# Batch 0 of a fused attention and MoE kernel: its second half in plain float32, and its weights converted over more steps

## The chip, the cores and the metric

The kernel is written for one core of a Trainium2 chip. The metric is the device time of one execution in microseconds (us). "TensorE" does the matrix products, "VectorE" and "ScalarE" the elementwise work, "GpSimd" a little of the rest; DMA transfers are started from the queue of SyncE (SP) and from GpSimd's.

## The reference

Three stages follow one another; B = 8 batches, 8 heads, 576 rows, 512 channels. Only the first two touch the change.

```python
proj = np.einsum('bhsd,df->bhsf', x, w_phi)           # x is q, then k
proj = proj - np.max(np.abs(proj), axis=-1, keepdims=True)
phi = np.concatenate([np.exp(proj), np.exp(-proj)], axis=-1)
...
kv = np.einsum('bhsf,bhsd->bhfd', k_p, v)
...
xk = mu_k * x + (1.0 - mu_k) * x_prev                 # x_prev: the row before
xr = mu_r * x + (1.0 - mu_r) * x_prev
k = np.maximum(xk @ w_k, 0.0)                         # 512 -> 1024
v = k * k @ w_v                                       # 1024 -> 512
r = 1.0 / (1.0 + np.exp(-(xr @ w_r)))                 # 512 -> 512
x = r * v
...
h = np.maximum(x @ w_in, 0.0)
...
return h * gate @ w_out
```

## The kernel before, in words

**Attention** runs in 32 blocks (`block(Pi)`), one for two heads of one batch; four blocks make a batch. In a block TensorE projects rows (`pk`, `pq`), turns tiles (`pt`, `px`, `pr`), sums keys with values (`pkv`) and makes the results (`pn`). VectorE takes the largest absolute value of each row (`mx`), subtracts it (`t`), and normalizes the results (`rd`, `xn`). ScalarE takes the exponentials (`kp`, `kr`, `qf`) and copies the turned results to `xT`.

**The MoE** (`moe(u)`) works on units: unit u is half of a batch, 288 rows, so batch 0 is units 0 and 1. A unit has 20 steps: eight of k (`psk`, four weight blocks of 128 by 128 each), and twice two of receptance (`psr`, four blocks each) and four of values (`psv`, two products of eight blocks each, and two steps in which VectorE multiplies). Its inputs are mixed from `xT` (`mix`: ScalarE scales, VectorE adds the scaled row before).

**Precision.** From unit 1 on, each weight block is multiplied three times in the reduced format fp32r (`mm3`): low weights by high inputs, high by low, high by high. Inputs, weights and squares of k must be split into high and low for that: a ScalarE copy rounds, a VectorE subtraction gives the rest (`ml`, `kl`, `split` for weights). Unit 0 takes one plain float32 matmul for each block, with the whole weight, which lies where the low half will be.

**The weights** arrive as float64 and are converted chunk by chunk, 20 chunks of 512 columns (`step`): SP loads `raw` (two buffers), ScalarE takes the high word (`h<-raw`), VectorE clamps, shifts and combines (four instructions, `h<-h`, `h<-h`, `h<-raw,h` twice), and SP moves the result to its place. `tick()` brings each chunk under way one stage further and starts the next. Ticks stand twice in each block from -1 to 6, at steps given by `WAT`, and in `want(n)`, which ticks until n + 2 chunks are ready.

**The order.** TensorE's instructions keep the order in which the code gives them; on the other engines a scheduler chooses the order. From block 4 on, `feed` hands MoE steps out between the blocks: 6, 6, 7 and 9 in blocks 4 to 7 (`SR`), then 10 in each. What is left of the MoE follows the last block, then the third stage.

Of the kernel before, what the change touches and what calls it, by code (L numbers as in the profile page):

```python
# [25 lines left out]

NS = 15

MS, SLOW, SR = 4, 8, {4: 6, 5: 6, 6: 7, 7: 9}

WAT = {4: (4, 10), 5: (3, 7, 11), 6: (3, 5, 7, 9)}
DS0 = 10
AHEAD = 2
HS = S // 2
V1 = D + 1

# [6 lines left out]
def fused_kernel(ctx: ExitStack, tc: tile.TileContext, qk, va, wphi, ones2, mu, wk, wv, wr, win, wout, cw, out):  # L43
# [33 lines left out]
    def f(x):  # L77
        return x.bitcast(F32)
# [78 lines left out]
    with ExitStack() as p1:  # L157
# [27 lines left out]
        def split(n=None):  # L185

            while n is None or cleft[0] < n:
                if half:
                    hs, ls = half.pop()
                    V.behind("tensor_tensor", ls, f(ls), f(hs), ALU.subtract)  # L190
                    cleft[0] += 1
                if whole and (n is None or cleft[0] < n):
# [5 lines left out]
        under, ready, whole, half, cleft = [], [0], [], [], [0]  # L198

        def tick():  # L200
            for at in (2, 1):
# [221 lines left out]
        def mix(u, j):  # L423

            b, hf = divmod(u, 2)
            o = hf * HS
            hi = main.tile([P, KC, HS], F32R if u else F32, tag="mh", bufs=2, name=f"mh{j}")
            if u == 0:
# [3 lines left out]
                return hi, hi  # L432
            lo = main.tile([P, KC, HS], F32R, tag="ml", bufs=2, name=f"ml{j}")
# [22 lines left out]

        def want(n):

            while ready[0] < min(n + AHEAD, 20):
                tick()  # L460

        def moe(u):
            b, hf = divmod(u, 2)

            def mm(ps, wh, wl, xh, xl, first, last):
                if u:
                    mm3(ps, wh, wl, xh, xl, first, last)
                else:
                    T.matmul(ps, f(wl), xh, start=first, stop=last)

            def need(n):
                want(n)
                if u:
                    split(n)
            o = hf * HS
            for j in range(2):
                while not mix_next(u, j):
                    yield
            xh, xl = mixed.pop((u, 0))
            k2 = []  # L480
            for fp in range(FC // 2):
                kf = tmps.tile([P, 2, HS], F32, tag="tmp", name="kf")
                for j in range(2):
                    ps = psm.tile([P, 512], F32, tag="mm", name="psk")[:, :HS]
                    fc = 2 * fp + j
                    need(fc + 1)
                    for c in range(KC):
                        w = slice(fc * DM + c * P, fc * DM + c * P + P)
                        mm(ps, wkh[:, w], wkl[:, w], xh[:, c], xl[:, c], c == 0, c == KC - 1)
                    A.activation(kf[:, j], ps, AF.Relu)  # L490
                    if u == 1:
                        split()
                    yield
                if u == 0:
                    kh = main.tile([P, 2, HS], F32, tag="kh", bufs=4, name="kh")
                    A.square(kh, kf)
                    k2.append((kh, kh))
                    continue
                if u == 1:
                    A.square(kf, kf)  # L500
                else:
                    V.tensor_tensor(kf, kf, kf, ALU.mult)
                kh = main.tile([P, 2, HS], F32R, tag="kh", bufs=4, name="kh")
                kl = main.tile([P, 2, HS], F32R, tag="kl", bufs=4, name="kl")
                A.copy(kh, kf)
                V.tensor_tensor(kl, kf, f(kh), ALU.subtract)
                k2.append((kh, kl))
            rh, rl = mixed.pop((u, 1))
            for mp in range(2):
                sg = main.tile([P, 2, HS], F32, tag="sg", bufs=1, name="sg")  # L510
                for j in range(2):
                    ps = psm.tile([P, 512], F32, tag="mm", name="psr")[:, :HS]
                    mc = 2 * mp + j
                    need(9 + 6 * mp + j)
                    for c in range(KC):
                        w = slice(mc * DM + c * P, mc * DM + c * P + P)
                        mm(ps, wrh[:, w], wrl[:, w], rh[:, c], rl[:, c], c == 0, c == KC - 1)
                    A.activation(sg[:, j], ps, AF.Tanh, scale=0.5)
                    if u == 1:
                        split()  # L520
                    yield
                mix_next(u + 1, mp)
                x2 = tmps.tile([P, 2, HS], F32, tag="tmp", name="x2")
                for j in range(2):
                    ps = psm.tile([P, 512], F32, tag="mm", name="psv")[:, :HS]
                    mc = 2 * mp + j
                    need(12 + 6 * mp + 2 * j)
                    for kc in range(FC):
                        w = slice(mc * DFF + kc * P, mc * DFF + kc * P + P)
                        kh, kl = k2[kc // 2]  # L530
                        mm(ps, wvh[:, w], wvl[:, w], kh[:, kc % 2], kl[:, kc % 2], kc == 0, kc == FC - 1)
                    if u < 2:
                        split()
                    yield
                    if u < 2:
                        split()
# [15 lines left out]
        load_v(1)  # L552

        def extras(Pi, n):
            if n in WAT.get(Pi, ()):
                tick()
            if Pi == 7 and n == 14:
                taps()
            if Pi >= DS0 and dsteps and n in (3, 11):
# [181 lines left out]
```

## Time and profile before

| | |
|---|---|
| median of 3 runs | 1233.19 us (1229.55 to 1234.22) |
| the profiled execution | 1230.63 us, of which the span of the trace is 1228.7 |
| mean granted clock of TensorE | 0.995 |
| busy in the span: TensorE, VectorE, ScalarE, GpSimd | 1207.6, 762.8, 697.2, 67.8 us |
| moved by DMA | 100.81 MB, 82 GB/s on the mean |

The time of the profiled execution is the span and what lies around it. An engine is busy while an instruction of it runs; the granted clock is 1.00 where TensorE runs at 2.4 GHz and 0.50 where it runs at 1.2 GHz.

### The profile page before, as it was taken

The numbers are of one execution on the slowest core, as the hardware profiler recorded it, in microseconds if no ns is written. First come the engines' busy times: TensorE is split into PE (matmuls) and PEld (weight loads), VectorE is DVE, ScalarE is ACT, GpSimd is POOL, SyncE is SP. The second block draws the span as 40 slices with busy tenths as digits, with TensorE's granted clock in tenths as the row PEclk, the third lists the DMA queues.
The fourth block names the chain that finished last, engine by engine and source line by source line (L and its number), as shares of the span: only waits on it lengthen the run. The fifth ranks groups of instructions, "written<-read, shape, count | busy, mean of one in ns | idle before, by whom it ended". The sixth has DMA issues, their size and how long they took to land.

```text
span 1228.7 us, 29049 instructions
## 1 busy us (share of the span) xinstructions
PE 1207.6 (98%) x11920; PEld 1139.4 (93%) x11920; DVE 762.8 (62%) x1584; ACT 697.2 (57%) x1644; POOL 67.8 (6%) x179
## 2 busy tenths in 40 slices
PE   7899999999999999999999999999999999999998
PEld 7778899999999999999999999998888888888887
DVE  7979776576765765767646534426555754475555
ACT  6766776565665664665645534426554655465554
POOL 0000000111110101111000000000000000000000
PEclk9989999999999999999999999999999999999999
DMA  6656213222322332333110004050122101210220
GB/s 205 220 188 205 94 42 89 86 92 77 120 78 84 105 111 85 93 86 104 50 52 22 12 21 157 20 188 8 55 63 62 32 32 63 62 44 20 63 62 31
DMA packets 58838, 100.81 MB, mean 82 GB/s; under 512 B 10321, under 2 KB 39121, under 8 KB 58705
## 3 DMA queue, kind: packets, MB, share of 16 engines
q1 hardware_dynamic: 45424, 73.41, 18.1%
q0 software_dynamic: 3920, 15.93, 4.4%
q10 hardware_dynamic: 9360, 9.61, 2.9%
q8 instruction: 94, 1.54, 0.5%
q14 instruction: 40, 0.32, 0.1%
HBM read 66.42 MB, written 27.26 MB: 76 GB/s over the span
## 4 chain that ended last, share of the span: by engine, by line
PE 90%; DVE 4%; DMA 3%; ACT 2%; issue 1%; SPq 0%; ACTq 0%
PE psh L150 5%; PE psh L152 5%; PE psh L151 5%; PE pkv L309 5%; PE psv L150 5%; PE psv L151 5%; PE psv L152 5%; PE psk L151 5%; PE psk L152 5%; PE psk L150 5%; PE pso L150 5%; PE pso L152 5%; PE pso L151 5%; PE pn L362 5%; PE psr L150 3%; PE psr L151 3%
## 5 line engine op out<-in xcount | busy, mean ns | idle before, releaser
L58 DVE SCALAR_TENSOR_TENSOR ct<-h,cw,ct 128x460 f32<-128x460 f32 (+2 forms) x160 | 111.4, 696 | 84.9 <-ACT ct L58 83.7
L150 PE MATMUL psv<-kh,wvl 128*128 128x288 f32 x480 | 141.9, 296 | 0.0
L151 PE MATMUL psk<-ml,wkh 128*128 128x288 f32 x480 | 141.6, 295 | 0.0
L151 PE MATMUL psv<-kl,wvh 128*128 128x288 f32 x480 | 141.5, 295 | 0.0
L152 PE MATMUL psk<-mh,wkh 128*128 128x288 f32 x480 | 141.5, 295 | 0.0
L152 PE MATMUL psv<-kh,wvh 128*128 128x288 f32 x480 | 141.5, 295 | 0.0
L150 PE MATMUL psk<-mh,wkl 128*128 128x288 f32 x480 | 140.9, 293 | 0.0
L152 PE MATMUL psh<-xh,wih 128*128 128x462 f32 (+1 forms) x320 | 118.9, 372 | 0.0
L151 PE MATMUL psh<-xl,wih 128*128 128x462 f32 (+1 forms) x320 | 118.8, 372 | 0.0
L151 PE MATMUL pso<-gl,woh 128*128 128x460 f32 (+1 forms) x320 | 118.0, 371 | 0.0
L152 PE MATMUL pso<-gh,woh 128*128 128x460 f32 (+1 forms) x320 | 118.0, 371 | 0.0
L58 ACT ACTIVATE kf<-psk 128x288 f32<-128x288 f32 x128 | 52.3, 408 | 108.1 <-PE psk L152 105.2
L150 PE MATMUL psh<-xh,wil 128*128 128x462 f32 (+1 forms) x320 | 107.4, 372 | 0.0
L150 PEld LDWEIGHTS psv<-kh,wvl 128*128 128x128 f32 x480 | 90.1, 188 | 0.8
L58 ACT ACTIVATE h<-psh 128x462 f32<-128x462 f32 (+3 forms) x128 | 47.9, 410 | 75.7 <-PE psh L152 74.5
L150 PEld LDWEIGHTS psk<-mh,wkl 128*128 128x128 f32 x480 | 90.2, 188 | 0.1
L151 PEld LDWEIGHTS psk<-ml,wkh 128*128 128x128 f32 x480 | 90.2, 188 | 0.0
L151 PEld LDWEIGHTS psv<-kl,wvh 128*128 128x128 f32 x480 | 90.2, 188 | 0.0
L152 PEld LDWEIGHTS psv<-kh,wvh 128*128 128x128 f32 x480 | 90.2, 188 | 0.0
L152 PEld LDWEIGHTS psk<-mh,wkh 128*128 128x128 f32 x480 | 90.2, 188 | 0.0
L58 DVE SCALAR_TENSOR_TENSOR x<-sg,psv 128x288 f32<-128x288 f32 x64 | 29.0, 453 | 95.9 <-PE psv L152 85.7
L58 DVE TENSOR_TENSOR kf<-kf 128x576 f32<-128x576 f32 x56 | 42.4, 758 | 74.1 <-ACT kf L58 74.1
(106 smaller groups left out, 2836.7 us busy)
## 6 DMA issues: line engine op xcount, KB each, us to landing
rqk<-qk POOLq DMA_DIRECT2D x27, 576.0 KB, 4.8
va<-va SPq DMA_DIRECT2D x32, 325.0 KB, 4.4
x2s<-x SPq DMA_DIRECT2D x32, 288.0 KB, 2.3
raw<-wk SPq DMA_DIRECT2D x8, 512.0 KB, 5.0
raw<-wv SPq DMA_DIRECT2D x8, 512.0 KB, 3.7
raw<-win SPq DMA_DIRECT2D x16, 256.0 KB, 2.9
raw<-wout SPq DMA_DIRECT2D x16, 256.0 KB, 3.0
x2r<-x2s ACTq DMA_DIRECT2D x16, 231.0 KB, 2.7
```

What stands on the lines that cost most here:

```text
L58: x = op(*a, **k)
L150: T.matmul(ps, wl, xh, start=first, stop=False)
L151: T.matmul(ps, wh, xl, start=False, stop=False)
L152: T.matmul(ps, wh, xh, start=False, stop=last)
L309: T.matmul(o[r:r + 64], k_[:, r:r + 64], v_, start=(i == 0), stop=(i == len(prods) - 1))
L362: T.matmul(pn[b_][64 * r:64 * r + 64, j], qf[h_][:, c, o:o + 64], kv[:, c, h_], start=(j == 0 and c == 0), stop=(j == 4 - b_ and c == 1))
```

## The change

Unit 1 takes plain float32 as unit 0 does, and the two units go together (`moe_first`): k of unit 0, k of unit 1, then for each pair of output chunks receptance and values of unit 0 and of unit 1. The squares of k of both units stay in SBUF, unit 0's in the tiles `kh` and unit 1's in `kl`. Neither unit splits anything. The weights are split into high and low behind their last plain use: chunks of k while the first pair of output chunks runs, and so on (`ripe`), the last during k of unit 2.

Ticks now stand once in blocks -1 to 4, a second time in blocks 2 and 3, and in `beat`, which before the MoE product s of batch 0 ticks until 6 + 0.6 s chunks are ready. `SR` is 7 in each of blocks 4 to 7.

```diff
-MS, SLOW, SR = 4, 8, {4: 6, 5: 6, 6: 7, 7: 9}
-
-WAT = {4: (4, 10), 5: (3, 7, 11), 6: (3, 5, 7, 9)}
+MS, SLOW, SR = 4, 8, {4: 7, 5: 7, 6: 7, 7: 7}
+
+PRE, RATE = 6, 0.6
...
-            if -1 <= Pi < 7:
+            if -1 <= Pi <= MS:
                 tick()
...
-            if -1 <= Pi < 7:
+            if Pi in (MS - 2, MS - 1):
                 tick()
...
-            while ready[0] < min(n + AHEAD, 20):
+            while ready[0] < min(n, 20):
                 tick()
+
+        steps_ = [0]
+
+        def plain(o, w, x):
+
+            n = len(x)
+            for c in range(n):
+                T.matmul(o, f(w[:, c * P:c * P + P]), x[c], start=c == 0, stop=c == n - 1)
+
+        def beat(n):
+
+            want(max(n + 1, int(PRE + RATE * steps_[0])))
+            steps_[0] += 1
+
+        def moe_first():
...
+            for u in range(2):
...
+                xk_ = mixed.pop((u, 0))[0]
+                for fp in range(FC // 2):
...
+                        beat(fc + 1)
+                        plain(ps, wkl[:, fc * DM:fc * DM + DM], [xk_[:, c] for c in range(KC)])
+                        A.activation(kf[:, j], ps, AF.Relu)
+                        yield
...
+            ripe[0] = 8
+            for mp in range(2):
+                for u in range(2):
+                    rf = mixed[u, 1][0]
...
+                        beat(9 + 6 * mp + j)
+                        plain(ps, wrl[:, mc * DM:mc * DM + DM], [rf[:, c] for c in range(KC)])
+                        A.activation(sg[:, j], ps, AF.Tanh, scale=0.5)
+                        split()
+                        yield
...
+                        beat(12 + 6 * mp + 2 * j)
+                        plain(ps, wvl[:, mc * DFF:mc * DFF + DFF], k2[u])
+                        split()
+                        yield
...
+                ripe[0] += 6
...
-            for u in range(2 * B):
+            for _ in moe_first():
+                yield
+            for u in range(2, 2 * B):
                 for _ in moe(u):
                     yield u
```

On TensorE, between blocks 6, 7 and 8, the end of unit 0 was followed by unit 1 in threes. `mh_1251`, `mh_1260` are unit 0's mixed inputs for k and receptance, `mh_1586` and `ml_1587` the halves of unit 1's for k; "..." stands for a whole attention block. Before:

```order
L469 MATMUL psv<-kh,wvl 128x288 x8
L469 MATMUL psr<-mh_1260,wrh 128x288 x8
L469 MATMUL psv<-kh,wvl 128x288 x16
...
L150 MATMUL psk<-mh_1586,wkl 128x288
L151 MATMUL psk<-ml_1587,wkh 128x288
L152 MATMUL psk<-mh_1586,wkh 128x288
```

Now the same stretch between blocks 5 and 8 reads so; `m_1215`, `m_1263` are the inputs for k of units 0 and 1, `m_1510`, `m_1567` those for receptance.

```order
L468 MATMUL psk<-m_1215,wkl 128x288 x4
L468 MATMUL psk<-m_1263,wkl 128x288 x24
...
L468 MATMUL psk<-m_1263,wkl 128x288 x8
L468 MATMUL psr<-m_1510,wrh 128x288 x8
L468 MATMUL psv<-kh,wvl 128x288 x16
...
L468 MATMUL psr<-m_1567,wrh 128x288 x8
```

Each weight block of unit 1 has moved from three instructions to one, and unit 1 from behind unit 0 to between its parts.

On VectorE, in block 0, from the keys' tile to the results, a chunk's conversion stood between the attention's rows. Before:

```order
L58 TENSOR_REDUCE mx<-pk 128x4 x2
L58 TENSOR_TENSOR t<-pk,mx 128x512 x2
L58 TENSOR_SCALAR h<-h 128x512
L58 TENSOR_REDUCE mx<-pq 128x4 x2
L58 TENSOR_SCALAR h<-h 128x512
L58 TENSOR_TENSOR t<-pq,mx 128x512 x2
L58 SCALAR_TENSOR_TENSOR h<-raw,h 128x512 x2
L58 TENSOR_SCALAR rd<-pn 128x5
```

Now:

```order
L57 TENSOR_REDUCE mx<-pk 128x4 x2
L57 TENSOR_TENSOR t<-pk,mx 128x512 x2
L57 TENSOR_REDUCE mx<-pq 128x4 x2
L57 TENSOR_TENSOR t<-pq,mx 128x512 x2
L57 TENSOR_SCALAR rd<-pn 128x5
```

The conversion has moved out of block 0; blocks 1 and 2 keep one each of two, blocks 3 and 4 two.

On VectorE, in block 2, from the keys' tile to the queries', now (`m_1215` to `m_1567` as above):

```order
L57 TENSOR_REDUCE mx<-pk 128x4 x2
L57 TENSOR_TENSOR t<-pk,mx 128x512 x2
L57 TENSOR_SCALAR h<-h 128x512
L57 SCALAR_TENSOR_TENSOR m_1215<-xT,mu_79,m_1215 128x288
L57 TENSOR_REDUCE mx<-pq 128x4 x2
L57 SCALAR_TENSOR_TENSOR m_1510<-xT,mu_79,m_1510 128x288
L57 TENSOR_SCALAR h<-h 128x512
L57 SCALAR_TENSOR_TENSOR m_1263<-xT,mu_79,m_1263 128x288
L57 SCALAR_TENSOR_TENSOR m_1567<-xT,mu_79,m_1567 128x288
L57 TENSOR_TENSOR t<-pq,mx 128x512 x2
```

Before, only the two mixes of unit 0 stood here (and in blocks 1, 3 and 4); unit 1's have moved forward to them from behind block 5.

## Rows read from the trace of the kernel before

**Rows 1.** The page: busy us, share, instructions; the chain's shares by engine.

```profile
PE 1207.6 (98%) x11920; PEld 1139.4 (93%) x11920; DVE 762.8 (62%) x1584; ACT 697.2 (57%) x1644; POOL 67.8 (6%) x179
PE 90%; DVE 4%; DMA 3%; ACT 2%; issue 1%; SPq 0%; ACTq 0%
```

**Rows 2.** Windows: stretch, its length, busy us (instructions) by engine, granted clock, DMA share.

```profile
8.07:73.92 65.85, 57.65 (x1078) 51.84 (x1078) 61.46 (x144) 48.16 (x124) 2.15 (x4) 0.92 0.61 199
73.92:176.00 102.08, 100.01 (x1135) 88.86 (x1132) 81.74 (x177) 72.34 (x174) 3.04 (x9) 1.00 0.43 138
176.00:575.00 399.00, 399.00 (x5122) 393.04 (x5122) 265.94 (x611) 239.22 (x620) 49.58 (x63) 1.00 0.30 90
```

**Rows 3.** Timeline of TensorE: start, length, instructions, idle before. The lower two bound 93 matmuls.

```profile
102.73 4.04 PE L469 MATMUL psv<-kh,wvl 128*128 128x288 f32 x16
106.61 0.60 PE L321 MATMUL px<-ident,xn 128*128 128x128 f32 x4
...
141.71 0.29 PE L150 MATMUL psk<-mh,wkl 128*128 128x288 f32 x1
...
153.87 0.29 PE L152 MATMUL psk<-mh,wkh 128*128 128x288 f32 x1
```

**Rows 4.** Timeline of VectorE in block 2: mixes, maxima, and a chunk's conversion.

```profile
44.43 0.94 DVE L58 SCALAR_TENSOR_TENSOR mh<-xT,mu,mh 128x288 f32<-128x288 f32 x2
45.29 0.68 DVE L58 TENSOR_REDUCE mx<-pq 128x4 f32<-128x512 f32 x1
45.89 0.41 DVE L58 TENSOR_SCALAR h<-h 128x512 uint32<-128x512 uint32 x1
46.22 1.28 DVE L58 TENSOR_TENSOR t<-pq,mx 128x512 f32<-128x512 f32 x2
47.42 0.68 DVE L58 SCALAR_TENSOR_TENSOR h<-raw,h 128x512 uint32<-128x512 uint32 x1
48.02 0.15 DVE L58 TENSOR_SCALAR rd<-pn 128x5 f32<-128x5 f32 x1
```

**Rows 5.** Groups of VectorE from 8 to 74 us: busy us, mean ns, idle before.

```profile
L58 DVE SCALAR_TENSOR_TENSOR h<-raw,h 128x512 uint32<-128x512 uint32 x18 | 12.3, 682 | 0.0
```

**Rows 6.** Waits of TensorE from 8 to 74 us: total, times, longest.

```profile
PE pk L252 <- DVE xn L58: 3.6, 4, 1.2
PE pk L252 <- ACT qf L58: 2.5, 3, 1.6
```

**Rows 7.** ScalarE from 8 to 74 us: its wait for raw chunks, and one in the timeline.

```profile
ACT h L58 <- DMA raw<-wk: 6.6, 3, 2.7
...
61.69 0.66 ACT L58 ACTIVATE h<-raw 128x512 f32<-128x512 f32 x1 [2.65 <-DMA raw<-wk]
...
62.70 2.07 ACT L58 ACTIVATE qf<-pt 128x512 f32<-128x512 f32 x4
```

**Rows 8.** Timeline of TensorE: fourteen of the keys' products in blocks 3 and 4.

```profile
50.83 1.16 PE L252 MATMUL pk<-wp,rqk 64*128 64x128 f32 x14 [0.29 <-ACT qf L58]
...
63.84 2.07 PE L252 MATMUL pk<-wp,rqk 64*128 64x128 f32 x14 [1.63 <-ACT qf L58]
```

**Rows 9.** DMA issues from 20 to 80 us: KB each, median us to landing.

```profile
raw<-wk SPq DMA_DIRECT2D x6, 512.0 KB, 4.0
```

**Rows 10.** Window of a stretch in block 4 with a lower granted clock.

```profile
62.50:69.80 7.30, 5.96 (x49) 5.18 (x51) 6.05 (x14) 5.24 (x15) 0.29 (x1) 0.53 0.39 117
```

**Rows 11.** Groups of VectorE from 74 to 176 us: splitting of mixed inputs.

```profile
L58 DVE TENSOR_TENSOR ml<-xf,mh 128x576 fp32r<-128x576 f32 x6 | 4.5, 750 | 0.5 <-ACT mh L58 0.4
```

**Rows 12.** Waits of TensorE from 74 to 176 us.

```profile
PE pkv L309 <- ACT qf L58: 1.1, 1, 1.1
PE pq L252 <- ACT qf L58: 0.4, 1, 0.4
```

**Rows 13.** Windows of block 3 and of block 7, as TensorE runs them.

```profile
47.86:58.63 10.77, 9.69 (x200) 8.62 (x196) 10.70 (x28) 9.61 (x26) 0.53 (x1) 1.00 0.60 195
...
132.72:141.21 8.49, 8.49 (x196) 8.13 (x194) 6.28 (x14) 5.86 (x17) 0.59 (x1) 1.00 0.43 134
```

More of the change, by code (lines that the diff above doesn't have):

```diff
@@ L191, in split @@
                     cleft[0] += 1
-                if whole and (n is None or cleft[0] < n):
+                if cleft[0] < (ripe[0] if n is None else n):
                     half.append(whole.pop(0))
@@ L196, in split @@
                     return
-        under, ready, whole, half, cleft = [], [0], [], [], [0]
+        under, ready, whole, half, cleft, ripe = [], [0], [], [], [0], [0]
         def tick():
@@ L426, in mix @@
             o = hf * HS
-            hi = main.tile([P, KC, HS], F32R if u else F32, tag="mh", bufs=2, name=f"mh{j}")
-            if u == 0:
+            if u < 2:
+                hi = main.tile([P, KC, HS], F32, tag=("mh", "ml")[j], bufs=2, name=f"m{j}")
                 for c in range(KC):
@@ L432, in mix @@
                 return hi, hi
+            hi = main.tile([P, KC, HS], F32R, tag="mh", bufs=2, name=f"mh{j}")
             lo = main.tile([P, KC, HS], F32R, tag="ml", bufs=2, name=f"ml{j}")
@@ L457, in want @@
         def want(n):
-            while ready[0] < min(n + AHEAD, 20):
+            while ready[0] < min(n, 20):
                 tick()
+        steps_ = [0]
[7 more added lines that the diff above has]
+        def moe_first():
+            while not mix_next(0, 0):
+                yield
+            k2 = [[], []]
+            for u in range(2):
+                while not mix_next(u, 0):
+                    yield
+                xk_ = mixed.pop((u, 0))[0]
+                for fp in range(FC // 2):
+                    kf = tmps.tile([P, 2, HS], F32, tag="tmp", name="kf")
+                    for j in range(2):
+                        ps = psm.tile([P, 512], F32, tag="mm", name="psk")[:, :HS]
+                        fc = 2 * fp + j
+                        beat(fc + 1)
+                        plain(ps, wkl[:, fc * DM:fc * DM + DM], [xk_[:, c] for c in range(KC)])
+                        A.activation(kf[:, j], ps, AF.Relu)
+                        yield
+                    kh = main.tile([P, 2, HS], F32, tag=("kh", "kl")[u], bufs=4, name="kh")
+                    A.square(kh, kf)
+                    k2[u] += [kh[:, 0], kh[:, 1]]
+                    if (u, fp) in ((0, 1), (0, 3), (1, 1)):
+                        mix_next(*{(0, 1): (1, 0), (0, 3): (0, 1), (1, 1): (1, 1)}[u, fp])
+            ripe[0] = 8
+            for mp in range(2):
+                for u in range(2):
+                    rf = mixed[u, 1][0]
+                    sg = main.tile([P, 2, HS], F32, tag="sg", bufs=1, name="sg")
+                    for j in range(2):
+                        ps = psm.tile([P, 512], F32, tag="mm", name="psr")[:, :HS]
+                        mc = 2 * mp + j
+                        beat(9 + 6 * mp + j)
[3 more added lines that the diff above has]
+                        yield
+                    if mp:
+                        mix_next(2, u)
+                    x2 = tmps.tile([P, 2, HS], F32, tag="tmp", name="x2")
+                    for j in range(2):
+                        ps = psm.tile([P, 512], F32, tag="mm", name="psv")[:, :HS]
+                        mc = 2 * mp + j
+                        beat(12 + 6 * mp + 2 * j)
+                        plain(ps, wvl[:, mc * DFF:mc * DFF + DFF], k2[u])
+                        split()
+                        yield
+                        split()
+                        V.scalar_tensor_tensor(x2[:, j], sg[:, j], 1.0, ps, ALU.add, ALU.mult)
+                        yield
+                    SY.dma_start(x2s[0][:, 2 * mp:2 * mp + 2, u * HS:u * HS + HS], x2)
+                ripe[0] += 6
+            for u in range(2):
+                mixed.pop((u, 1))
@@ L462, in moe @@
         def moe(u):
             b, hf = divmod(u, 2)
[L465 to L474, printed above, removed]
             o = hf * HS
@@ L485, in moe @@
                     fc = 2 * fp + j
-                    need(fc + 1)
+                    split(fc + 1)
                     for c in range(KC):
                         w = slice(fc * DM + c * P, fc * DM + c * P + P)
-                        mm(ps, wkh[:, w], wkl[:, w], xh[:, c], xl[:, c], c == 0, c == KC - 1)
+                        mm3(ps, wkh[:, w], wkl[:, w], xh[:, c], xl[:, c], c == 0, c == KC - 1)
                     A.activation(kf[:, j], ps, AF.Relu)
-                    if u == 1:
+                    if u == 2:
                         split()
                     yield
[L494 to L502, printed above, removed]
+                V.tensor_tensor(kf, kf, kf, ALU.mult)
                 kh = main.tile([P, 2, HS], F32R, tag="kh", bufs=4, name="kh")
@@ L513, in moe @@
                     mc = 2 * mp + j
-                    need(9 + 6 * mp + j)
+                    split(9 + 6 * mp + j)
                     for c in range(KC):
                         w = slice(mc * DM + c * P, mc * DM + c * P + P)
-                        mm(ps, wrh[:, w], wrl[:, w], rh[:, c], rl[:, c], c == 0, c == KC - 1)
+                        mm3(ps, wrh[:, w], wrl[:, w], rh[:, c], rl[:, c], c == 0, c == KC - 1)
                     A.activation(sg[:, j], ps, AF.Tanh, scale=0.5)
-                    if u == 1:
-                        split()
                     yield
@@ L526, in moe @@
                     mc = 2 * mp + j
-                    need(12 + 6 * mp + 2 * j)
+                    split(12 + 6 * mp + 2 * j)
                     for kc in range(FC):
@@ L530, in moe @@
                         kh, kl = k2[kc // 2]
[L531 to L533 removed]
+                        mm3(ps, wvh[:, w], wvl[:, w], kh[:, kc % 2], kl[:, kc % 2], kc == 0, kc == FC - 1)
                     yield
[L535 to L536 removed]
                     V.scalar_tensor_tensor(x2[:, j], sg[:, j], 1.0, ps, ALU.add, ALU.mult)
@@ L541, in moe_all @@
         def moe_all():
-            for u in range(2 * B):
+            for _ in moe_first():
+                yield
+            for u in range(2, 2 * B):
                 for _ in moe(u):
@@ L554, in extras @@
         def extras(Pi, n):
-            if n in WAT.get(Pi, ()):
-                tick()
             if Pi == 7 and n == 14:
```

1 line of the change is left out of this document (removed).

## The prediction, made before the result was known

> **What bounds the kernel now.** I read the busy shares and the chain of work first, then the span cut into stages, then what TensorE waits for in each. TensorE is busy for 1207.6 of 1228.7 us and holds 90% of the chain [rows 1]. By stage [rows 2]: from 176 to 575 us, and all but the same before and after, it has no idle time at all, so whatever matrix work is added to the program is paid in full and idle time can be won back only early. The early part has two stages. From 8.07 to 73.92 us (attention blocks 0 to 4, no MoE work yet) TensorE is busy for 57.65 of 65.85 us, and VectorE for 61.46, 93%: VectorE is the bound there. From 73.92 to 176 us (batch 0's MoE between the blocks) TensorE is idle for 2.1 us and VectorE is busy for 81.7 of 102.1. So the change is a trade: what it does to TensorE's work after 74 us, against what it does to VectorE's work before.
>
> **The added matrix work.** The second part of batch 0 (unit 1) has 32 + 16 + 32 = 80 weight blocks. Before, each costs three reduced-precision matmuls; now one plain float32 one, which the trace records as two pieces. Both forms stand in this trace. Plain: 16 pieces from 102.73 to 106.61 us, 242.5 ns each, 485 ns a block. Three-matmul form: 92 starts from 141.71 to 153.87 us, 132.2 ns each, 396.5 ns a block [rows 3]. The granted clock is 1.00 in both. The difference is 88.5 ns, times 80 blocks: **+7.1 us**, in a stage where TensorE hardly waits. So the step that looks like a saving (one call for three) is a cost. The length of one three-matmul row, 0.29 us, holds the overlap with its neighbours; the distance between starts is what the span pays.
>
> The Trainium skill (FP8 and Floating Point Precision, TensorE Precision Notes) says that true float32 takes four passes through the array. By four passes of 288 columns at 2.4 GHz against three it would be 480 against 360 ns, an estimate from that page, and +9.6 us for the 80 blocks. The plain row agrees within 5 ns; the three-matmul row is 36 ns slower than its passes, so the sum goes by the rows. By the page the time would be 2.5 us more, 1239.5 us; as both forms are measured in this trace, it gets no chance of its own.
>
> **What leaves VectorE early.** Converting one chunk of weights costs it two shifts/clamps of 0.33 us and two combining steps of 0.60 us, by their starts: 1.86 us [rows 4]. Before, nine chunks are converted between 8 and 74 us (18 combining steps) [rows 5]; the order of the changed program has six ahead of the first MoE matmul. Three fewer: -5.6 us. But the scheduler pulls the scaling of batch 0's second half forward into blocks 1 to 4: two more of the scaling steps in each, 0.43 us by their starts [rows 4], eight in all: +3.4 us. The balance for VectorE is -2.1 us, by block -1.9, -1.0, -1.0, +0.9, +0.9. TensorE's first MoE matmul follows block 4's last product, at 73.92 us, so it comes forward by what the stage gets shorter.
>
> How much of that arrives? Of TensorE's 8.2 us of idle time there, 3.6 are waits for VectorE's normalized tile and 2.5 for ScalarE's query features [rows 6]. ScalarE's share is not VectorE's load: ScalarE stood three times for a raw weight chunk, 6.6 us in all; at 61.69 us it had stood 2.65 us, with the query features queued behind [rows 7], and TensorE's next products waited 1.63 us for these [rows 8]. Chunk loads land in about 4 us [rows 9] into two buffers, and a load starts when the chunk two before is converted. With fewer chunks in blocks 0 and 1 the third chunk's buffer comes free later in block 1, so a ScalarE wait of this kind moves to block 2 and block 3; behind it stand the copies of the transposed column and four scalings, and behind these VectorE's. I price that at 1.3 us a block, an estimate: half of the longest such wait, because VectorE has other work ready for about that long. In block 4 the wait of 2.65 us goes, since its chunk is loaded early. These about cancel.
>
> The clock matters too. In block 4 the granted clock is 0.53 from 62.5 to 69.8 us [rows 10], so 6.9 of these 7.3 us passed at 1.2 GHz, right behind that wait; fourteen products take 2.07 us there and 1.16 in block 3 [rows 8]. If block 4 no longer waits, up to half of that, 3.4 us, could come back; if the wait merely moves, the fall may move with it.
>
> Bounds for the early stage: nothing comes forward and one chunk wait is added, +1 us; or all of the 5.6 us of conversions comes forward, the scalings hiding in VectorE's gaps, -5.6 us. I take **-2 us**, the balance of VectorE's work, because that engine is 93% busy in the stage and the ScalarE terms point both ways.
>
> **The stage with batch 0's MoE.** Three chunks (+5.6 us) come into it, eight scalings (-3.4) and the splitting of unit 1's inputs and hidden values leave it: four subtractions of 0.75 us for the inputs [rows 11] and four of the same size for k squared, -6.0 us, and as many copies on ScalarE. VectorE's load falls by nearly 4 us, and TensorE's stage gets 7 us longer, so VectorE does not become the bound. The weights do not come late either: six chunks are ready when the k steps begin, a step lasts 4 x 0.485 = 1.94 us, one chunk per 1.67 steps means one in 3.2 us, and the second half's eight k steps need no new weights at all, so the lead grows from 6 to over 7 while k of both halves runs. The squares of k, eight tiles now, take both sets of four that the high and low halves of later units use, so nothing waits for a buffer. The pairs of output chunks change the order of products, not their number. Most of TensorE's idle 2.1 us here were two waits of 1.1 and 0.4 us for ScalarE's query features [rows 12]. I leave them as they are; bounds -2 us (all gone) and +3 us (a chunk wait of ScalarE holding up results in each of three blocks). New rates of MoE steps (7, 7, 7, 7 for 6, 6, 7, 9) give 28 steps by block 8 in both, so all behind it stays. Cost 0; its cover is TensorE's own full queue.
>
> **Sum.** +7.1 - 2.0 + 0 = **+5.1 us**; ends -0.5 and +11. The profiled execution took 1230.6 us (span 1228.7 and 1.9 around it), 2.6 below the median of 1233.2: 1235.7 by the one, 1238.3 by the other. I forecast 1237 us. A change under 0.5%, 6.2 us, can't be told from none here.
>
> **Rivals.**
> *The early stage becomes TensorE's.* If block 0's relief keeps every block ahead, the 8.2 us of idle time [rows 2] and the loss at half clock (granted 0.92 over the 65.85 us [rows 2], so 10.5 us at 1.2 GHz and 5.3 us lost) go: -13.5 + 7.1 = -6.4 us, 1224.2 by the profiled run, faster. For it: block 0's conversion goes altogether, and four of the waits in [rows 6] are for a tile that the conversions delay. Against it: VectorE was busy for 10.70 of block 3's 10.77 us and gets 0.9 more there, while a block without waits takes TensorE 8.49 us [rows 13]. Half of it, -6.7 + 7.1, would end at no change. 0.15 for this direction, 0.04 of it beyond 0.5%.
> *The chunk waits win (slower by over 0.5%).* One mechanism: ScalarE, in order, stands for a raw chunk with results behind it. It decides once what comes forward early is under 0.9 us, for then +7.1 stays above 6.2. With nothing won early and +3 us in the MoE stage: +10, 1240.7 by the profile, 1243 by the median. For it: the 2.65 us wait did reach TensorE [rows 7, 8], and VectorE's blocks 3 and 4 get longer, not shorter. Against it: the load on both engines falls after 74 us. 0.30.
> *The forecast itself*, +3 to +7: 0.55, of which 0.05 lies over 6.2 us.
> So faster 0.04, same 0.11 + 0.50 = 0.61, slower 0.35. The range takes in half of the first rival and most of the second: 1231 to 1242.5.
>
> **What would show it.** Right: 160 plain pieces more on the line of plain float32 and 240 three-matmul ones fewer, 242 and 132 ns between starts, the clock at 1.00; the first MoE matmul near 72 us; six chunks converted before it; every attention block from the tenth on about 5 us later than before. Wrong: a first MoE matmul before 69 us (then the first rival), or TensorE's waits after 74 us above 4 us, with ScalarE's chunk waits just ahead of them (the second); or plain pieces further apart than 243 ns.

## The result, and the profile after

The changed kernel takes 1242.45 us (median of 6 runs, 1241.70 to 1245.53) against 1231.45 (6 runs) for the kernel before: a ratio of 1.0093, 95% interval 1.0075 to 1.0112, so slower by over 0.5%. The forecast was no measurable change at 1237 us. The profiled execution has a span of 1239.9 us, 11.2 more than before. The page of the changed kernel, busy us and the chain's shares:

```profile
PE 1216.7 (98%) x11840; PEld 1140.2 (92%) x11840; DVE 758.7 (61%) x1576; ACT 692.4 (56%) x1636; POOL 66.8 (5%) x179
PE 89%; ACT 4%; DVE 3%; DMA 3%; issue 1%; ACTq 0%; SPq 0%
```

TensorE has 80 matmul records fewer (240 gone, 160 plain pieces come) and is busy 9.1 us longer [rows 1]. The windows of the three stages, cut at the first MoE matmul:

```profile
8.07:71.30 63.23, 55.23 (x1078) 49.92 (x1079) 57.94 (x137) 49.33 (x129) 3.12 (x8) 0.95 0.54 174
71.30:176.00 104.70, 100.97 (x1047) 84.92 (x1044) 74.28 (x164) 62.66 (x154) 2.46 (x5) 0.98 0.47 153
176.00:575.00 399.00, 398.55 (x5028) 389.08 (x5027) 266.08 (x607) 236.68 (x608) 46.86 (x62) 1.00 0.29 89
```

Against [rows 2]: the early stage is 2.6 us shorter, but the stage with batch 0's MoE has 3.7 us of idle time where it had 2.1, and part of it ran at 1.2 GHz (granted 0.98 on the mean, 1.00 before). TensorE's timeline shows where:

```profile
71.30 13.85 PE L468 MATMUL psk<-m,wkl 128*128 128x288 f32 x56
...
88.26 1.16 PE L251 MATMUL pk<-wp,rqk 64*128 64x128 f32 x14 [0.83 <-ACT xT L57]
89.24 1.16 PE L251 MATMUL pq<-wp,rqk 64*128 64x128 f32 x16
...
94.89 13.85 PE L468 MATMUL psk<-m,wkl 128*128 128x288 f32 x56
108.58 0.60 PE L320 MATMUL px<-ident,xn 128*128 128x128 f32 x4
...
113.91 1.68 PE L251 MATMUL pk<-wp,rqk 64*128 64x128 f32 x14 [2.89 <-ACT xT L57]
115.47 2.08 PE L251 MATMUL pq<-wp,rqk 64*128 64x128 f32 x16
```

The plain pieces run as forecast: 56 from 94.89 to 108.58, 242 to 243 ns between starts in all seven products, but for one 346 right behind the attention block (244 on the mean). In block 6 TensorE then stands 2.89 us for ScalarE's copy to `xT` and runs the queries' sixteen products in 2.08 us, where block 5's take 1.16 us (rows at 89.24 and 115.47): the granted clock is 0.50 from 114.4 to 117.8 us. ScalarE (ACT), VectorE (DVE) and SP around that copy:

```profile
106.93 1.42 DVE L57 SCALAR_TENSOR_TENSOR h<-raw,h 128x512 uint32<-128x512 uint32 x2
108.95 0.53 SPq L170 DMA_DIRECT2D raw<-wv  x1
108.88 0.69 ACT L57 ACTIVATE kf<-psk 128x288 f32<-128x288 f32 x2
112.72 0.66 ACT L57 ACTIVATE h<-raw 128x512 f32<-128x512 f32 x1 [3.15 <-DMA raw<-wv]
113.28 0.57 ACT L57 COPY xT<-px 128x512 f32<-128x512 f32 x1
```

VectorE frees a raw buffer at 108.3, SP issues the next load at 108.95, it lands at 112.6, and ScalarE, in order, stands for it 3.15 us with the copy to `xT` next in its queue.

The start of a block's results (`pn`) tells where blocks stand against before, in us: block 4 -2.6, block 5 0.0, block 6 +5.9, block 8 +3.2, block 10 +5.9, block 16 +7.4, block 31 +10.5. What lies behind block 31's start adds 0.7. So the difference keeps growing behind batch 0's MoE, where the forecast had it constant.

### The profile page after: what moved, and what is told of

It is laid out like the page before. It is cut to its first block, busy times and chain, and to the rows that moved or that the text cites. A ratio compares the mean times of both kernels' runs of the same rounds, so it can differ in the third digit from the quotient of the medians.

```text
span 1239.9 us, 28895 instructions
## 1 busy us (share of the span) xinstructions
PE 1216.7 (98%) x11840; PEld 1140.2 (92%) x11840; DVE 758.7 (61%) x1576; ACT 692.4 (56%) x1636; POOL 66.8 (5%) x179
## 4 chain that ended last, share of the span: by engine, by line
PE 89%; ACT 4%; DVE 3%; DMA 3%; issue 1%; ACTq 0%; SPq 0%
PE psh L149 5%; PE psh L151 5%; PE psh L150 5%; PE pkv L308 5%; PE pso L149 5%; PE psv L149 5%; PE pso L151 5%; PE pso L150 5%; PE psv L150 5%; PE psk L149 5%; PE psv L151 5%; PE psk L150 5%; PE psk L151 5%; PE pn L361 4%; PE psv L468 3%; PE psr L150 2%
## 5 line engine op out<-in xcount | busy, mean ns | idle before, releaser
L149 PE MATMUL psk<-mh,wkl 128*128 128x288 f32 x448 | 132.9, 297 | 0.0
L150 PE MATMUL psv<-kl,wvh 128*128 128x288 f32 x448 | 132.8, 297 | 0.0
L149 PE MATMUL psv<-kh,wvl 128*128 128x288 f32 x448 | 132.5, 296 | 0.0
L150 PE MATMUL psk<-ml,wkh 128*128 128x288 f32 x448 | 132.1, 295 | 0.0
L151 PE MATMUL psk<-mh,wkh 128*128 128x288 f32 x448 | 132.0, 295 | 0.0
L151 PE MATMUL psv<-kh,wvh 128*128 128x288 f32 x448 | 132.0, 295 | 0.0
L57 ACT ACTIVATE kp<-t 128x512 f32<-128x512 f32 x128 | 70.1, 618 | 37.4 <-PE pkv L308 22.1
L149 PE MATMUL pso<-gh,wol 128*128 128x460 f32 (+1 forms) x320 | 88.0, 371 | 0.9 <-ACT gh L57 0.9
L57 DVE TENSOR_TENSOR g<-h,ct 128x460 f32<-128x460 f32 (+3 forms) x128 | 54.4, 457 | 50.8 <-ACT ct L57 49.9
L149 PEld LDWEIGHTS psk<-mh,wkl 128*128 128x128 f32 x448 | 84.2, 188 | 0.8
```

What stands on the lines that cost most here:

```text
L57: x = op(*a, **k)
```

## Experiments

**Theory.** The 11.2 us are 7 of plain float32, 3 from a MoE step that slips behind batch 0, and a wait at block 6 that eats what the early stage wins; the rest is scatter. The rivals: plain float32 costs more than its pieces; the spread of the ticks, or SP's queue, is the cause of the wait; the late growth is a loss in later units. The kernel before ran beside all of them, with medians of 1230.6 to 1231.7 us.

### The slipped step

`feed` keeps its credit as a running float sum. With 7/15 in blocks 4 to 7 the credit is 0.0 when block 8 begins, and after nine steps the fifteen additions of 10/15 in block 8 leave 0.9999999999999997, short of the tenth: nine steps come in place of ten, and everything behind is one step late. Version `e1`:

```diff
-                while credit[0] >= 1:
+                while credit[0] >= 0.999:
```

> The changed kernel, with one edit: the counter that hands MoE steps out between blocks fires at 0.999 instead of 1. In the changed kernel rounding of the sums of 7/15 loses one step, so block 8 gets 9 steps where the kernel before gives 10, and from there each unit is cut by the attention blocks one step earlier in its order. Theory A (the cut costs): from block 10 on TensorE loses 0.3 us in each pair of blocks against the kernel before, 3 us by the end; with 268 steps as before, pairs of blocks take 48.95 us again and the span falls from 1239.9 to about 1236.5. Theory B (the steps' cut is harmless, the later loss belongs to the changed data or weights): no change, 1239 to 1240.

Measured: 1240.06 us, ratio 1.0070 (1.0045 to 1.0094), span 1237.1. From block 11 to block 31 every start is 7.31 or 7.32 us behind before. The starts of blocks 14 and 16 in TensorE's timelines, of the kernel before, the changed one and `e1`, with two rows between them:

```profile
308.01 2.27 PE L362 MATMUL pn<-kvf,qf 128*64 128x65 f32 x72
356.96 2.27 PE L362 MATMUL pn<-kvf,qf 128*64 128x65 f32 x72
```

```profile
315.07 2.27 PE L361 MATMUL pn<-kvf,qf 128*64 128x65 f32 x72
324.65 0.40 PE L150 MATMUL psv<-kl,wvh 128*128 128x288 f32 x1
360.77 1.26 PE L251 MATMUL pq<-wp,rqk 64*128 64x128 f32 x16
364.33 1.86 PE L361 MATMUL pn<-kvf,qf 128*64 128x65 f32 x58
```

```profile
315.32 2.27 PE L361 MATMUL pn<-kvf,qf 128*64 128x65 f32 x72
360.92 1.06 PE L251 MATMUL pq<-wp,rqk 64*128 64x128 f32 x16
364.27 1.92 PE L361 MATMUL pn<-kvf,qf 128*64 128x65 f32 x60
```

Two blocks take 48.95 us before and here, 49.26 in the changed kernel. The 0.31 us are two stalls too short to be listed as waits: 0.20 in the queries' products of block 15 (1.26 for 1.06 us) and 0.10 in a product of values (0.40 for 0.29 us), which the profile puts down to VectorE's low half of the squares of k. The difference to `e1` is 0.3 us at block 8, before the slip has an effect, and 10.49 - 7.32 = 3.2 us at block 31: the slip costs 2.9 us. The growth of 0.31 us a pair holds from block 12 to block 25. The same slip in the kernel before (nine steps in block 8):

```diff
-MS, SLOW, SR = 4, 8, {4: 6, 5: 6, 6: 7, 7: 9}
+MS, SLOW, SR = 4, 9, {4: 6, 5: 6, 6: 7, 7: 9, 8: 9}
```

> The kernel before, with 9 steps instead of 10 in block 8, as rounding makes it in the changed kernel; nothing else is touched. Theory A (the cut of the units by the attention blocks costs 0.3 us in each pair of blocks from 10 on): +3 us, a span near 1232. Theory B (the cost needs the changed kernel's unit order): 1228.5 to 1229.

Measured: 1233.19 us (10 runs), ratio 1.0019 (1.0008 to 1.0031), span 1230.8. The lag grows by 0.31 us a pair of blocks, from 0.00 at block 13 to +1.87 at block 25 (+2.06 at block 31). Ahead of the slip it was -0.30, so the slip costs 2.4 us here: it costs in both kernels, with or without plain float32.

### The price of plain float32

```diff
+                if u == 10:
+                    T.matmul(ps, f(wh), f(xh), start=first, stop=last)
-                if u:
+                elif u:
                     mm3(ps, wh, wl, xh, xl, first, last)
```

> The kernel before, with a single edit: unit 10 (batch 5, in the steady stage) takes one plain float32 matmul of the high halves for each of its 80 weight blocks in place of three reduced-precision ones; the products with its low halves are left out. Nothing else moves: same steps, same ticks, same splits. It prices the plain blocks by themselves. Theory A (the term of +7.1 us is a pure TensorE cost of 80 x 88.5 ns): the blocks ahead of unit 10 start as before, each attention block behind it 7.1 us later than before, span about 1228.7 + 7.1 = 1235.8 us, if the early stage falls as it did in the profile of before. Theory B (plain pieces cost more when they stand beside ScalarE's and VectorE's steady work, or the longer TensorE stage hides part of it): a shift under 6 or over 8.5 us between the blocks ahead of unit 10 and those behind it.

Measured: 1239.14 us, ratio 1.0067 (1.0047 to 1.0086), span 1238.0. Starts of blocks 25 and 29 here, then before:

```profile
579.06 1.16 PE L362 MATMUL pn<-kvf,qf 128*64 128x65 f32 x34
...
684.73 2.27 PE L362 MATMUL pn<-kvf,qf 128*64 128x65 f32 x72
```

```profile
577.22 2.27 PE L362 MATMUL pn<-kvf,qf 128*64 128x65 f32 x72
...
676.12 2.27 PE L362 MATMUL pn<-kvf,qf 128*64 128x65 f32 x72
```

The lag goes from 1.84 to 8.61 us: 6.8 us for 80 blocks, 85 ns each (forecast 88.5). The Trainium skill's rule of four passes for true float32 (FP8 and Floating Point Precision, TensorE Precision Notes), set against three, made an estimate of +9.6 us; the run's blocks lie 2.8 us under it, and agree with the rows instead. The times alone could not tell: their interval is 5.8 to 10.6 us more than before. The 1.84 arose by block 7, ahead of the edit: executions differ there (below).

Next, the kernel before with unit 1 in plain float32 and its splits behind its plain use, but with unit 1 behind unit 0 and the old ticks:

```diff
-            if u == 0:
+            if u < 2:
...
-                if u:
+                if u > 1:
                     mm3(ps, wh, wl, xh, xl, first, last)
...
+            if u == 1:
+                ripe[0] = 8
...
+                if u == 1:
+                    ripe[0] += 6
```

> The kernel before, with unit 1 in plain float32 and nothing else moved: the two units stay one after the other, the ticks stay, the weights are split behind unit 1's last plain use. It takes the plain matmuls alone. Theory A: +7.1 us for 80 blocks at 88.5 ns, less some tenths for the splitting of inputs that goes, so a span of 1235 to 1236.5 against 1228.7. Theory B (plain float32 is dearer than its distance between starts, or the early conversions matter little): +10 us or more, a span of 1239 or above.

Measured: 1242.29 us, ratio 1.0079 (1.0056 to 1.0102), span 1239.9. Theory A missed. Block 6 is 1.4 us late and block 12 11.1; of the 9.7 between, 7 are the pieces and the rest waits that before has not, the longest at the turn from receptance to values in this kernel's timeline:

```profile
127.73 8.03 PE L469 MATMUL psv<-kh,wvl 128*128 128x288 f32 x32 [1.98 <-DVE x L58]
```

B's number came, through other waits than it named: this order of units doesn't get plain float32 cheaper.

### Does the early gain arrive?

Both kernels once more, unedited.

> The kernel before, unedited, profiled again. It asks how far the early stage varies by itself. Theory A (the place of the stretches at 1.2 GHz differs between executions of one program and sets its length): the first MoE matmul comes at another time than 73.92 us, anywhere from 70 to 74 us, and the stretches at a granted clock near 0.5 lie elsewhere than at 39 to 42 and 63 to 70 us, while TensorE's block from the tenth on starts within 1 us of before. Theory B (the early stage is the same in each execution and what the experiments showed there is due to their edits): first MoE matmul at 73.9 us within 0.3 us, stretches at the same places.

> The changed kernel, unedited, profiled again, for the same question as the repeat of before. Theory A: the first MoE matmul comes at another time than 71.30 us, by over 0.5 us, with its stretch at 1.2 GHz elsewhere; the late start of block 6 (5.9 us behind before) stays, since the wait of TensorE for the copy to xT there belongs to the program: 2 to 3 us of wait near 114 us. Theory B (block 6's wait came from the place of the clock's fall in that one execution): no wait over 1 us there and block 6 at most 4 us behind before.

Measured: before 1231.16 us, span 1229.2; after 1242.19 us, span 1240.4. The repeat of before, TensorE's timeline:

```profile
70.22 1.97 PE L469 MATMUL psk<-mh,wkl 128*128 128x288 f32 x7
...
85.85 1.16 PE L252 MATMUL pk<-wp,rqk 64*128 64x128 f32 x14 [1.42 <-ACT xT L58]
...
111.11 2.09 PE L309 MATMUL pkv<-va,kp 128*64 128x65 f32 x64 [2.30 <-ACT qf L58]
...
131.16 2.21 PE L469 MATMUL psv<-kh,wvl 128*128 128x288 f32 x8 [1.25 <-DMA wvl<-h]
```

The same program's first MoE matmul comes 3.7 us sooner (73.92 in the first profile), with one stretch at 1.2 GHz (51.1 to 54.5 us) where the first had two (39.0 to 42.4 and 62.9 to 69.7). And nothing of it arrives: the waits in these rows, for ScalarE and for a chunk, are 5.0 us, where the first profile has 1.1 us at the second place [rows 12], none at the first and 0.2 at the third:

```profile
PE psv L469 <- DMA wvl<-h: 0.2, 1, 0.2
```

Block 7 starts 0.5 us later than in the first profile, as theory A had it. The repeat of the changed kernel was within 1.3 us of its first profile in every block, its wait at block 6 3.38 us: that one belongs to the program, so theory A holds there, but its early stage did not vary as A had it (first MoE within 0.4 us).

A stronger form: the kernel before without its second tick in blocks -1 to 1, and with four ticks at steps of blocks 4 and 5 each.

```diff
-WAT = {4: (4, 10), 5: (3, 7, 11), 6: (3, 5, 7, 9)}
+WAT = {4: (3, 6, 9, 12), 5: (3, 6, 9, 12), 6: (3, 5, 7, 9)}
...
-            if -1 <= Pi < 7:
+            if 2 <= Pi < 7:
                 tick()
```

> The kernel before (unit 1 in threes), with three ticks moved: no second tick in blocks -1, 0 and 1, one more each in blocks 4 to 6. It takes the thinner early conversion alone. Theory A (VectorE's work sets blocks 0 to 4): three conversions of 1.86 us less there, the first MoE matmul at 70 to 72 us instead of 73.9; the chunks fall into block 4 and 5's feeds, where ScalarE may stand for them: span 1225 to 1228. Theory B (those blocks are set by chunk waits and the clock, which merely move): within 1.5 us of 1228.7.

Measured: 1241.58 us, ratio 1.0085 (1.0064 to 1.0106), span 1238.8. Its first MoE matmul comes at 66.62 us and block 4 is 7.3 us ahead of before, with no stretch at 1.2 GHz until then; block 7 is 10.0 us behind. Both theories missed the span. Waits of TensorE from 66 to 176 us in it:

```profile
PE psv L469 <- DMA wvl<-h: 6.9, 3, 2.7
PE pq L252 <- ACT qf L58: 3.2, 2, 2.8
```

A conversion not made early is waited for in the MoE stage. The changed kernel with fewer chunks per step, in the other direction:

```diff
-PRE, RATE = 6, 0.6
+PRE, RATE = 6, 0.45
```

> The changed kernel, with RATE 0.45 instead of 0.6: one chunk in 4.3 us of k steps instead of one in 3.2. Theory A: chunks come at no less than 4 to 5 us apart there, because a load stands in SP's queue behind the store of the chunk before it, so at 0.6 ScalarE stands for raw chunks ahead of the copy of the transposed column; at 0.45 the 2.9 us wait in block 6 goes, with the 1.2 GHz stretch behind it: span 1235.5 to 1237. Theory B: the wait is of another kind (the copy itself is late): no change, or the chunks of the second half now come late and cost more.

Measured: 1253.63 us, ratio 1.0175 (1.0154 to 1.0196), span 1250.9. Block 8 is 0.6 us ahead of before, block 9 17.8 behind; waits from 74 to 260 us:

```profile
PE psv L468 <- DMA wvl<-h: 6.6, 3, 3.2
PE pq L251 <- ACT qf L57: 3.0, 1, 3.0
PE psv L468 <- DVE h L57: 2.5, 1, 2.5
```

The second row is block 6's wait, 2.96 us up to 110.72 us: theory A missed, for it stays with the chunks further apart. The waits for values are 9.1 us together, all between 166.9 and 185.7 us; from 169.5 to 190 us the granted clock was 0.75 on the mean, so half of those 20.5 us passed at 1.2 GHz.

### The wait at block 6

The changed kernel with the old ticks (its diff undone in those places):

> The changed kernel, with the conversion's ticks of the kernel before (two in each block from -1 to 6, the extra ones in blocks 4 to 6, and two chunks ahead of need). Theory A: the first MoE matmul goes back from 71.3 to about 74 us (+2.6), and the waits for the transposed column in blocks 5 and 6, 0.8 and 2.9 us with the lower clock behind them, go (-4.5): a span of 1237 to 1239. Theory B (the spread conversion is no loss): +2.6 and nothing back, 1242 or above.

Measured: 1244.14 us, ratio 1.0099 (1.0075 to 1.0123), span 1242.0. The wait stays in block 6, one result further, and so does the stretch at 1.2 GHz (115.8 to 122.6):

```profile
116.51 2.08 PE L252 MATMUL pq<-wp,rqk 64*128 64x128 f32 x16 [2.65 <-ACT qf L58]
```

The spread of the ticks is not the cause. Then the stores of converted chunks on GpSimd's queue, with the slipped step given back:

```diff
-            SY.dma_start(f(ls[:, o_]), h)
+            G.dma_start(f(ls[:, o_]), h)
```

> The changed kernel with the step counter mended (as in the first experiment, span 1237.1), and the stores of converted weight chunks issued from GpSimd's queue instead of SP's. Theory A (a raw load stands in SP's queue behind the store of the chunk before, which waits for VectorE): loads start as soon as a buffer is free, ScalarE's 2.8 us wait ahead of block 6's copy falls to under 1 us, span 1233 to 1235. Theory B (the buffer, not the queue, holds the load back; or block 5 itself holds the conversions): the wait stays at 2 us or more, span 1236 to 1238.

Measured: 1243.53 us, ratio 1.0107 (1.0086 to 1.0128); the profiled execution was a long one, span 1245.4. The wait grows, though SP now issues the load at 111.74 us, within 0.1 us of the end of the conversion that frees its buffer (0.6 us in `e1`). So the buffer, and not SP's queue, holds the load back, and theory B holds in that. The span doesn't compare well, since block 5 is 3.2 us late here already.

TensorE's waits for the copy, from 74 to 176 us:

```profile
PE pk L251 <- ACT xT L57: 5.2, 3, 3.5
```

Then the same version without the stores' edit, holding back the chunk that is asked for at the end of block 5's steps, so that the scheduler puts the copy to `xT` ahead of it:

```diff
-            want(max(n + 1, int(PRE + RATE * steps_[0])))
+            s = steps_[0]
+            want(max(n + 1, int(PRE + RATE * (s if s < 9 or s > 15 else 9 if s < 14 else 11.7))))
```

> The changed kernel with the step counter mended (1237.1), and no new chunk in the last four steps of block 5's feed; the two held back come in the next two steps. In the order of ScalarE the chunk that stood right ahead of block 6's copy of the transposed column now stands behind it. Theory A (that chunk's wait is what TensorE waits for in block 6, and the 1.2 GHz stretch follows from it): block 6's 2.8 us wait and most of its 1.2 GHz stretch go, 3 to 5 us, span 1232.5 to 1234.5. Theory B (block 6 is late for another reason, or the wait moves to the weights of the values): less than 1.5 us comes back, or a wait of TensorE for a weight chunk takes its place.

Measured: 1238.19 us, ratio 1.0058 (1.0038 to 1.0079), span 1235.6: the lowest median of the change's complete forms, though its interval overlaps that of `e1`. TensorE at block 6 in `e1`, then here:

```profile
113.27 1.67 PE L251 MATMUL pk<-wp,rqk 64*128 64x128 f32 x14 [2.76 <-ACT xT L57]
```

```profile
109.92 1.06 PE L251 MATMUL pk<-wp,rqk 64*128 64x128 f32 x16
```

ScalarE here in block 6 and in block 7:

```profile
108.51 0.59 ACT L57 COPY xT<-px 128x512 f32<-128x512 f32 x1
...
109.58 0.66 ACT L57 ACTIVATE h<-raw 128x512 f32<-128x512 f32 x1
...
133.06 0.68 ACT L57 ACTIVATE h<-raw 128x512 f32<-128x512 f32 x1 [4.04 <-DMA raw<-wr]
133.65 0.57 ACT L57 COPY xT<-px 128x512 f32<-128x512 f32 x1
```

Block 6 is 0.6 us late where it was 5.2 with the slipped step alone given back: the place of the copy is the cause there. No stretch at 1.2 GHz is left before the program's end. But in block 7 a chunk wait of 4.04 us now stands ahead of the copy, and TensorE waits there for query features (1.31 us) and again ahead of block 8 (1.23 us, no releaser shown), where `e1` has no wait. From block 12 on 1.3 of the 4.6 us are left (6.02 behind before, 7.31 in `e1`). So of theory A the wait and the stretch went, and its 3 to 5 us did not come.

Last, raw loads of half the size, in the kernel before and in the version of `e1`:

```diff
-            SY.dma_start(raw, src[:, o_])
+            SY.dma_start(raw[:, :256], src[:, o:o + 256])
```

> The kernel before, with raw weight chunks of half the size (256 KB in place of 512 KB): each of the 20 chunks loads only its first 256 columns, and ScalarE and VectorE convert those twice to fill 512 columns, in as many instructions of the same size. The other half of the weights is left out of the computation. The scheduler, which knows the shorter load, may place conversions a little differently. Theory A (the time in which a raw chunk lands, with two buffers, paces the stage from 68 to 139 us, so that what the early stage wins is given back there): ScalarE's waits for raw chunks of 2 to 4.5 us fall under 1 us, TensorE's waits between 74 and 140 us (1.7 us in the first profile of before, 5.7 us in its second) under 1 us, and block 7 starts 2 to 4 us ahead of 139.0 us, all behind it likewise; span 1225 to 1227 us. Theory B (VectorE's and ScalarE's own work paces it): block 7 within 0.7 us of 139.0 us and the span within 1 us of 1228.7 us.

> The changed kernel with the lost step given back (the threshold of 0.999) and the same half-sized raw chunks; the other half of the weights is left out. Theory A (block 6 is late in the changed kernel because ScalarE stands for a raw chunk ahead of the copy to xT): the wait of 2.8 us at block 6 goes or falls under 0.8 us, no stretch at 1.2 GHz follows it, blocks from the twelfth on start 2 to 4 us ahead of the version with the lost step alone given back (so 3.3 to 5.3 us behind before in place of 7.3), span 1233 to 1235 us. Theory B (the place in ScalarE's order or VectorE's work is the cause, and the length of the load is not): a wait of over 1.5 us stays at block 6 and the blocks from the twelfth on start within 1 us of that version, span 1236 to 1238 us.

Measured: 1235.56 us, ratio 1.0037 (1.0027 to 1.0047), span 1235.4; and 1235.78 us, 1.0038 (1.0026 to 1.0051), span 1233.8. A load takes 3.0 us in place of 4.0. In the changed kernel the wait falls from 2.76 to 1.75 us, no stretch at 1.2 GHz follows, and blocks from the twelfth on start 2.2 us sooner: between the theories, nearer A. TensorE and ScalarE at block 6 in it:

```profile
112.03 1.16 PE L255 MATMUL pk<-wp,rqk 64*128 64x128 f32 x14 [1.75 <-ACT xT L57]
110.55 0.66 ACT L57 ACTIVATE h<-raw 128x512 f32<-128x512 f32 x1 [3.44 <-DMA raw<-wv]
111.40 0.58 ACT L57 COPY xT<-px 128x512 f32<-128x512 f32 x1
```

In the kernel before both theories missed: block 7 is 6.6 us late. With the shorter load the scheduler put a conversion ahead of block 6's copy, and it stood 2.43 us. The profile names VectorE's mix, which ended at 114.25 us, but the chunk itself, issued at 111.40 us, had landed only at 114.22: it stood for both. Half loads first, then before, where the copy goes ahead of the conversion:

```profile
114.33 0.66 ACT L58 ACTIVATE h<-raw 128x512 f32<-128x512 f32 x1 [2.43 <-DVE xf L58]
114.89 0.57 ACT L58 COPY xT<-px 128x512 f32<-128x512 f32 x1
```

```profile
107.25 0.59 ACT L58 COPY xT<-px 128x512 f32<-128x512 f32 x1
...
110.03 0.67 ACT L58 ACTIVATE h<-raw 128x512 f32<-128x512 f32 x1 [1.21 <-DVE xf L58]
```

TensorE waited 3.0 us for that copy, 1.2 GHz followed from 117.0 to 120.4 us, and the lag grew from 2.6 us at block 5 to 7.4 at block 6. So an edit that shortens each load by a quarter made the kernel slower: 4.8 of these 7.4 us came with one position in ScalarE's queue, and the 2.6 ahead of it were there by block 4.

## Why the prediction was wrong

Two steps failed: that equal step counts leave everything behind block 8 as it was, and that the MoE stage costs nothing because TensorE's own full queue covers it.

**Plain float32, +7.1 us: right.** 6.8 us by itself, in a unit without any other edit.

**"28 steps by block 8 in both, so all behind it stays": wrong, 2.9 us.** The counts by block 8 are right, but in block 8 the float credit stops short of its tenth step, and the MoE runs one step late to the end. The prediction counted steps only up to block 8 and took equal counts for an equal order. A single step behind it looked free, with TensorE busy without a gap; it costs 0.31 us per pair of blocks from block 12 to 25. What stalls the queries' products in this phase is not settled.

**Early stage, -2 us: the size near on the mean, not clear of scatter; the use of it wrong.** The first MoE matmul comes at 71.30 us, 2.6 sooner than in the first profile of before. That this pair fits the forecast is in part luck, for the same early part varies from one execution to the next: 73.92, 70.22, 75.16, 70.14 and 73.76 us in before, its repeat and its versions with unit 1 in plain float32, with the slip and with unit 10 in plain float32, whose orders on VectorE and ScalarE are the same until 97 us; 71.30, 71.69, 70.74 and 68.69 in the changed kernel, its repeat, `e1` and the version with the hold. The means, 72.6 and 70.6, are 2.0 us apart, and the ranges overlap. The sum, besides, took what the stage gets shorter as gained. In both profiles of before, whose first MoE matmuls are 3.7 us apart, block 7 starts within 0.5 us; in the thinned version 7.3 us won at block 4 were lost by block 7. The stage from 74 to 140 us uses up an early lead in waits for converted chunks and for the ScalarE work behind them.

**MoE stage, 0: wrong; a wait of the size of its upper bound came.** The second rival named the mechanism, ScalarE in order before a raw chunk with results behind it, and its price of +3 us: 2.89 us at block 6, and a stretch at 1.2 GHz in which 30 products took 3.64 us from the first start to the last end, 1.50 more than the 2.14 they take in block 5. TensorE's waits after 74 us were 3.7 us here and 4.2 in the repeat, on either side of the 4 us that the prediction named as the sign of this rival. Its cover, "TensorE's own full queue", was not there: the queue is in order, the keys' products wait for the copy to `xT`, and all other matrix work stands behind them. That VectorE's and ScalarE's load falls was true (74.28 us of VectorE against 81.74) and did not matter, for the copy was late by its place in a queue, not by load: with the copy ahead, in the version with the hold, block 6's wait is gone.

Early stage and MoE stage together come to about +0.2 us in place of -2.0 (7.31 from block 11 on in `e1`, less 7.1). That is one execution against one, and four executions with before's program up to block 7 lie between -0.30 and +1.83 us there, so it is known to a microsecond or two only. With it the sum would have been +7.3 with the step in place, on the slow side of the bound of 6.2 us, as `e1` measured (1.0070). The slip alone, on top of the forecast's +5.1, would have passed that bound too. The slip's 2.9 and the 0.3 by which the first profile was behind `e1` ahead of it make +10.5 at block 31, and 0.7 behind block 31's start make 11.2. That rest is scatter: 509.2 us in both profiles of before and in the repeat of the changed kernel, 510.0 in its first profile, 510.3 in `e1`.

The measured 1242.45 us lies just inside the stated range of 1231 to 1242.5 us. That is luck: the range's upper part stood for chunk waits with nothing won early, and the slipped step was in no term of it.

No form of the change beat the kernel before: three reduced-precision matmuls are cheaper than a plain one, and what plain float32 frees (splitting, on VectorE and ScalarE) lies in the stage behind 71 us, where VectorE is busy for 74.28 of 104.70 us; no run here turned it into time.

What stays open: what paces the stage from 74 to 140 us in the kernel before. Shorter loads could not tell, since the scheduler's order moved with them. A third raw buffer was not tried.

## What to carry to other kernels

A gain ahead of a stage that is fed by a pipeline counts only once one has looked where that stage's own supplies would make it wait: compare two profiles of the same program, if they happen to start the stage at different times, and take a shift of the early stage as won only against several executions. On an engine that runs in order, look at what stands right ahead of the one instruction that the bounding engine needs; its load says nothing about that. A rate kept as a running float sum should be checked for the step it loses, since a phase that slips by one lasts to the end.

## What was not expected of the hardware

The same program's early stage ended at 73.92 us in one execution and at 70.22 in another, with 10.2 and 3.4 us at a granted clock of 0.50; the whole took the same time (spans 1228.7 and 1229.2). Between 74 and 200 us, in all profiles here, a stretch at 1.2 GHz of 3.4 us or more lay in or within 2 us behind every wait of TensorE of 2.65 us or more (ten of them, in the changed kernel, its repeat, `e1`, the versions with the old ticks, with RATE 0.45, with the stores on GpSimd's queue, the thinned one and half loads before). Of shorter ones some had it (2.46 us in the thinned version) and some not (2.48 in the version with the hold, 1.75 in half loads after), so this is what these runs have, and no rule. Block 6's wait of 2.89 us in the changed kernel came to 4.4 with the clock behind it (2.89 + 1.50).
